# One weight load of a decode layer cut in two: seven rows for all partitions, the eighth by loads of 96, 25 and 7 partitions

## The chip, the cores and the metric

The kernel runs on one core of a Trainium2 chip. The metric is the device time of one execution in microseconds (us), taken as the median of several runs. Inputs and weights lie in HBM; everything that is computed on has to be brought into SBUF (128 partitions) by DMA first. The core has 16 DMA engines that share this work.

## The reference

One layer of a transformer decodes one new token for each of 4 sequences (hidden size D = 1024):

```
h  = x + attention(layernorm(x)) @ wo     # 32 heads of 128, 4 kv heads, the last 2048 cached positions
h2 = h + (silu(n @ w1) * (n @ w3)) @ w2   # n = layernorm(h), F = 3584
```

with q = layernorm(x) @ wq, softmax(q k^T / sqrt(128)) v per head, and everything stored in bfloat16. wq and wo are 1024 x 4096 and 4096 x 1024 (8 MB each), w1, w3 and w2 are 1024 x 3584 or 3584 x 1024 (7 MB each), the part of the k and the v cache that is read is 8 MB each. With 4 tokens per weight the work is nearly all reading: the trace counts 55.58 MB read from HBM.

## The kernel before

All big tensors pass through one SBUF tile, `ring` (128 partitions x 5 units of 16384 bfloat16), in which `at(unit, ...)` gives views: `wq_s` at unit 0, `k_s` at 3, the v blocks at 2 and 0, `wo_s` at 3, `w1_s` at 1, `w3_s` at 3, and w2 in five blocks of 13, 8, 4, 2 and 1 rows from unit 0 on. A view is overwritten by the next tensor as soon as its last reader is done, so a load may have to wait for compute.

Every load goes through `load(dst, src)` (L124), a DMA issued by SyncE (SP). SP issues them in program order: wq in two pieces, four of k, four of v, wo, w1 (L432), w3, w2 in blocks. The program order is written by hand (`tc.manual_schedule()`); each load waits for the readers of the place that it overwrites and, as eight DMA semaphores are used in turn, for an earlier load on the same semaphore.

The weights are spread so that each partition holds whole rows of a matrix:

```
w1_v = B_w1.rearrange("(p kc) f -> p kc f", kc=KC)
w1_s = at(1, KC, F)
...
load(w1_s, w1_v)
```

With KC = 8, partition p holds rows 8p to 8p+7 of w1, each 3584 values or 7168 bytes, in HBM one run of 57344 bytes. The matmuls of `up_projection` (L494) go over kc from 0 to 7, and over each half of the columns in turn; `up_projection(w1_s, ...)` makes the gate, `up_projection(w3_s, ...)` the other factor. The load of w1 stands behind `output(1)`, whose matmuls (L381) are the last readers of the v blocks that lay in w1's place.

At the end the blocks of w2 arrive one by one and are multiplied as they come: the first two into `early_ps` (L538), the last three, of which the one-row block is loaded in two halves, into `y2_ps` (L554, called y_ps in the profile). Then `res` is made (L577, L578, L582) and stored by four small DMAs (L587), two from SP and two from ScalarE.

Of the kernel before, what the change touches and what calls it, by code (L numbers as in the profile page):

```python
# [10 lines left out]
P = 128  # L11
# [10 lines left out]
def kernel(  # L22
# [29 lines left out]
    KC = D // P  # L52
# [27 lines left out]
    w1_v = B_w1.rearrange("(p kc) f -> p kc f", kc=KC)  # L80
# [17 lines left out]
    def at(unit, *shape):  # L98
        o = unit * UNIT
        view = ring[:, o : o + int(np.prod(shape))]  # L100
        if len(shape) == 1:
            return view
        names = "abc"[: len(shape)]
        return view.rearrange(
            f"p ({' '.join(names)}) -> p {' '.join(names)}", **dict(zip(names, shape))
        )
# [5 lines left out]
    w1_s = at(1, KC, F)  # L112
# [10 lines left out]
    def load(dst, src):  # L123
        nc.sync.dma_start(out=dst, in_=src)  # L124
# [216 lines left out]
    def spread(b):  # L341

        P4 = ktpool.tile([P, JR * L5, Hkv], BF16, tag="P4")
        nc.vector.tensor_tensor(  # L344
            out=P4[:],
            in0=stage.pop(("p1", b))[:].rearrange("p (x o) -> p x o", o=1).to_broadcast([P, JR * L5, Hkv]),
            in1=gmask[:].to_broadcast([P, JR * L5, Hkv]),
            op=ALU.mult,
        )
        stage[("P4", b)] = P4  # L350
# [22 lines left out]
    def output(b):  # L373
        PT = stage.pop(("PT", b))
        o_ps = (
            small[:, 0].rearrange("p (j d) -> p j d", j=JM)
            if b % 2
            else ps.tile([P, JM, Dh], FP32, tag="ktA", name="o_ps")[:]
        )
        for i in range(JR // JM):  # L380
            nc.tensor.matmul(  # L381
                o_ps,
                lhsT=PT[:, i * JM : (i + 1) * JM, :].rearrange("p j h -> p (j h)"),
                rhs=v_s[b][:, i * JM : (i + 1) * JM, :],
                start=(i == 0),
                stop=(i == JR // JM - 1),
            )
        od = act.tile([P, JM, Dh], FP32, tag="od", bufs=1)
        nc.vector.scalar_tensor_tensor(  # L389
            out=od[:],  # L390
            in0=o_ps,
            scalar=rinv[:, b : b + 1],
            in1=jmask[:].to_broadcast([P, JM, Dh]),
            op0=ALU.mult,
            op1=ALU.mult,
        )
        o2 = act.tile([P, 2, Dh], FP32, tag="o2", bufs=1)
        nc.gpsimd.tensor_tensor(out=o2[:], in0=od[:, :2], in1=od[:, 2:], op=ALU.add)  # L398
        nc.gpsimd.tensor_tensor(out=om[:, b], in0=o2[:, 0], in1=o2[:, 1], op=ALU.add)
# [29 lines left out]
    spread(2)  # L429
    transpose_p(2)  # L430
    output(1)
    load(w1_s, w1_v)  # L432
    spread(3)
    transpose_p(3)
    total(1)
# [111 lines left out]
    for k in range(2):  # L547
        part = h1[2 * R * k : 2 * R * k + 2 * R, :]
# [25 lines left out]
    for k in range(2):  # L574
        part = slice(2 * R * k, 2 * R * k + 2 * R)
# [44 lines left out]
```

## Time and profile before

| | |
|---|---|
| median of 3 runs | 138.7 us (138.65 to 138.75) |
| the profiled execution's own time | 138.7 us |
| its span, first to last instruction | 136.7 us |
| mean granted TensorE clock | 0.912 |
| read from HBM, rate over the span | 55.58 MB, 407 GB/s |
| DMA share of the chain that ended last | 59% |
| PE busy, DVE busy, ACT busy | 74.8, 49.9, 28.8 us |

The 2.0 us between the span and the time lie before the first and after the last profiled instruction. A time in the text such as 133.61 is counted from the start of the span. The profile says of each DMA how many packets it took, and each packet's start, length and size; it does not say which of the 16 engines carried a packet. A load raises its semaphore once for each engine that worked on it, when that engine's share has landed; these times are in the trace as well.

### The profile page before, as it was taken

The numbers are of one execution on the slowest core, as the hardware profiler recorded it, in microseconds if no ns is written. First come the engines' busy times: TensorE is split into PE (matmuls) and PEld (weight loads), VectorE is DVE, ScalarE is ACT, GpSimd is POOL, SyncE is SP. The second block draws the span as 40 slices with busy tenths as digits, with TensorE's granted clock in tenths as the row PEclk, the third lists the DMA queues.
The fourth block names the chain that finished last, engine by engine and source line by source line (L and its number), as shares of the span: only waits on it lengthen the run. The fifth ranks groups of instructions, "written<-read, shape, count | busy, mean of one in ns | idle before, by whom it ended". The sixth has DMA issues, their size and how long they took to land.

```text
span 136.7 us, 1762 instructions
## 1 busy us (share of the span) xinstructions
PE 74.8 (55%) x762; PEld 40.6 (30%) x762; DVE 49.9 (37%) x50; ACT 28.8 (21%) x32; POOL 15.3 (11%) x41
## 2 busy tenths in 40 slices
PE   0000044959999986029966875994184000946471
PEld 0000011439957852014423323341042000413240
DVE  0000110006526363989799920004100594090022
ACT  3000130025968495104000000000405400000000
POOL 7300060000000000000176333000200000000000
PEclk9999999999999999955999999599959955599999
DMA  4999697999999999998978979969799798999960
GB/s 163 497 454 538 269 537 307 432 417 451 408 432 436 412 436 408 436 585 360 556 326 364 556 326 475 520 285 537 336 470 508 302 520 372 384 423 432 384 245 2
DMA packets 2795, 55.70 MB, mean 408 GB/s; under 512 B 324, under 2 KB 612, under 8 KB 740
## 3 DMA queue, kind: packets, MB, share of 16 engines
q1 hardware_dynamic: 2752, 55.58, 95.3%
q8 instruction: 6, 0.10, 0.3%
q10 hardware_dynamic: 36, 0.01, 0.0%
q14 instruction: 1, 0.01, 0.0%
HBM read 55.58 MB, written 0.01 MB: 407 GB/s over the span
## 4 chain that ended last, share of the span: by engine, by line
DMA 59%; PE 28%; DVE 6%; ACT 3%; SPq 1%; issue 1%; DVEq 0%
DMA ring<-in_B_w_dram 43%; DMA ring<-in_A_wq_dram 15%; PE kt_ps L267 9%; PE sc_ps L290 5%; PE q_ps L233 4%; PE o_ps L381 4%; PE gate L494 3%; DVE P L344 2%; DVE PT L366 2%; ACT ring L271 1%; PE small L381 1%; DVE ring L269 1%; SPq L124 1%; DVE rmax L302 1%; ACT q_sb L243 1%
## 5 line engine op out<-in xcount | busy, mean ns | idle before, releaser
L271 ACT COPY ring<-kt_ps 128x2048 bf16<-128x2048 bf16 x8 | 14.6, 1866 | 7.1 <-PE kt_ps L267 7.1
L267 PE MATMUL kt_ps<-ident,ring 128*128 128x128 bf16 x256 | 15.0, 219 | 0.6 <-DVE Qm L253 0.5
L267 PEld LDWEIGHTS <-ring 128*128 128x128 bf16 x256 | 14.4, 98 | 2.6 <-issue 2.6
L269 DVE COPY ring<-kt_ps 128x2048 bf16<-128x2048 bf16 x8 | 9.8, 1225 | 9.3 <-PE kt_ps L267 9.3
L398 POOL TENSOR_TENSOR o<-od 128x256 f32<-128x256 f32 x4 | 6.8, 1695 | 54.2 <-DVE od L389 54.2
L193 PE MATMUL sums_ps<-both,mean_f 128*128 128x64 f32 x4 | 1.1, 366 | 18.9 <-ACT both L191 18.9
L494 PE MATMUL up<-ring,n_T 128*32 128x448 bf16 x64 | 4.7, 467 | 12.2 <-DMA ring<-in_B_w_dram 12.2
L494 PEld LDWEIGHTS <-n_T 128*32 128x32 bf16 x128 | 4.2, 121 | 20.2 <-DMA ring<-in_B_w_dram 12.7
L344 DVE TENSOR_TENSOR P<-p,gmask 128x2048 bf16<-128x2048 bf16 x4 | 9.1, 2278 | 0.8 <-ACT p L331 0.8
L381 PEld LDWEIGHTS <-PT 128*128 128x128 bf16 x64 | 6.7, 107 | 9.0 <-issue 1.9
L366 DVE STREAM_TRANSPOSE PT<-P 128x2048 bf16<-128x2048 bf16 x4 | 9.2, 2306 | 0.1
L515 DVE RECIPROCAL eg<-eg 128x896 f32<-128x896 f32 x1 | 5.8, 5753 | 9.5 <-ACT eg L514 9.5
L468 PE MATMUL y_ps<-ring,oP 128*32 128x512 bf16 x64 | 8.8, 442 | 0.1
L233 PE MATMUL q_ps<-ring,n_T 128*32 128x512 bf16 x64 | 6.6, 587 | 3.8 <-DMA ring<-in_A_wq_dram 2.0
L381 PE MATMUL o_ps<-ring,PT 128*128 128x512 bf16 x32 | 8.6, 430 | 0.0
L290 PE MATMUL sc_ps<-ring,Qm 128*32 128x512 bf16 x64 | 7.6, 604 | 0.4 <-DVE ring L269 0.4
L538 PE MATMUL early_ps<-ring,hg_T 128*32 128x512 bf16 x42 | 4.9, 379 | 5.1 <-DMA ring<-in_B_w_dram 5.1
L381 PE MATMUL small<-ring,PT 128*128 128x512 bf16 x32 | 7.2, 379 | 0.7 <-DVE rinv L362 0.7
L193 PEld LDWEIGHTS sums_ps<-both,mean_f 128*128 128x128 f32 x4 | 0.8, 248 | 19.4 <-issue 16.9
L494 PE MATMUL gate<-ring,n_T 128*32 128x448 bf16 x64 | 4.6, 458 | 3.2 <-DMA ring<-in_B_w_dram 3.2
L577 ACT CAST res<-y_ps 64x128 bf16<-64x128 f32 x1 | 0.3, 259 | 26.3 <-PE y_ps L554 26.3
L218 DVE STREAM_TRANSPOSE x_T<-x_nat 128x256 bf16<-128x256 bf16 x1 | 0.6, 626 | 13.0 <-DMA x_nat<-in_A_x_dram 13.0
(81 smaller groups left out, 62.5 us busy)
## 6 DMA issues: line engine op xcount, KB each, us to landing
ring<-in_B_w_dram SPq DMA_DIRECT2D x2, 7168.0 KB
ring<-in_A_k_cache_dram SPq DMA_DIRECT2D x4, 2048.0 KB, 25.6
ring<-in_A_v_cache_dram SPq DMA_DIRECT2D x4, 2048.0 KB, 42.9
ring<-in_A_wq_dram SPq DMA_DIRECT2D x1, 7168.0 KB, 21.2
ring<-in_B_w_dram SPq DMA_DIRECT2D x1, 3328.0 KB
ring<-in_B_w_dram SPq DMA_DIRECT2D x1, 2048.0 KB
ring<-in_A_wq_dram SPq DMA_DIRECT2D x1, 1024.0 KB, 4.6
ring<-in_B_w_dram SPq DMA_DIRECT2D x1, 1024.0 KB, 28.1
```

What stands on the lines that cost most here:

```text
L233: nc.tensor.matmul(q_ps[R * c : R * c + R, hf], lhsT=xn_T[:, kc, :], rhs=wq_s[:, kc, o : o + HALF * Dh], start=(kc == 0), stop=(kc == KC - 1),
L267: nc.tensor.transpose(out=kt_ps[:, jj], in_=blocks[:, jj, :], identity=ident[:])
L269: nc.vector.tensor_copy(out=blocks, in_=kt_ps[:])
L271: nc.scalar.copy(out=blocks, in_=kt_ps[:])
L290: nc.tensor.matmul(sc_ps[b // 2][R * q : R * q + R, b % 2], lhsT=Qm[:, b, g * R : (g + 1) * R], rhs=kT[:, b, g, q], start=(g == 0), stop=( ...
L344: nc.vector.tensor_tensor(out=P4[:], in0=stage.pop(("p1", b))[:].rearrange("p (x o) -> p x o", o=1).to_broadcast([P, JR * L5, Hkv]), in1=g ...
L366: nc.vector.transpose(out=PT[:].rearrange("p j h -> p (j h)"), in_=stage.pop(("P4", b))[:].rearrange("p x g -> p (x g)"),)
L381: nc.tensor.matmul(o_ps, lhsT=PT[:, i * JM : (i + 1) * JM, :].rearrange("p j h -> p (j h)"), rhs=v_s[b][:, i * JM : (i + 1) * JM, :], star ...
L398: nc.gpsimd.tensor_tensor(out=o2[:], in0=od[:, :2], in1=od[:, 2:], op=ALU.add)
L468: nc.tensor.matmul(y_ps[R * i : R * i + R], lhsT=oP[:, t, :], rhs=row[:, i], start=False, stop=(t == T - 1), tile_position=(0, R * i), ski ...
L494: nc.tensor.matmul(out_ps[hf][R * c : R * c + R, :], lhsT=hn_T[:, kc, :], rhs=cols[:, kc, c, hf], start=(kc == 0), stop=(kc == KC - 1), ti ...
L515: nc.vector.reciprocal(out=eg[:], in_=eg[:])
```

## The change

Rows 0 to 6 of every partition of w1 come by one load, row 7 by three loads, for partitions 0 to 95, 96 to 120 and 121 to 127. All four are issued by SP where the one load was. The bytes, their places and the readers are the same.

```
@@ -429,7 +429,9 @@
     spread(2)
     transpose_p(2)
     output(1)
-    load(w1_s, w1_v)
+    load(w1_s[:, : KC - 1], w1_v[:, : KC - 1])
+    for part in (slice(0, 96), slice(96, 121), slice(121, P)):
+        load(w1_s[part, KC - 1 :], w1_v[part, KC - 1 :])
     spread(3)
     transpose_p(3)
     total(1)
```

On the other engines the order of instructions stays as it was; SP has three DMA issues more, between the first piece of w1 and w3. The eight DMA semaphores are taken in turn, so the loads and stores behind w1 use a semaphore three places further on than before.

More of the change, by code (lines that the diff above doesn't have):

```diff
@@ L431 @@
     output(1)
-    load(w1_s, w1_v)
+    load(w1_s[:, : KC - 1], w1_v[:, : KC - 1])
+    for part in (slice(0, 96), slice(96, 121), slice(121, P)):
+        load(w1_s[part, KC - 1 :], w1_v[part, KC - 1 :])
     spread(3)
```

## The prediction

> **What bounds the kernel now.** I read the chain that ended last first, in order of time; its columns are start, length and what.
>
> ```profile
> 68.72 30.62 DMA ring<-in_B_w_dram
> 99.34 0.14 issue
> 99.48 4.64 PE gate L494 x55
> ...
> 104.96 28.65 DMA ring<-in_B_w_dram
> 133.61 0.04 issue
> 133.65 0.30 PE y_ps L554 x2
> 133.95 0.02 issue
> 133.97 0.43 DVE res L582
> ```
>
> The end hangs on the landing of the last half row of w2 at 133.61. The load was issued 28.65 us earlier and stood in the queue all that time: the second piece of the chain is a queue, not a transfer. So the question is when the DMA engines get through their work. The windows say how full they are (last two columns: share of 16 engines, GB/s).
>
> ```profile
> 60.00:80.00 20.00, 15.10 (x64) 6.70 (x65) 17.19 (x13) 1.56 (x4) 7.42 (x6) 0.88 1.02 440
> 80.00:97.00 17.00, 11.89 (x84) 5.27 (x82) 2.44 (x5) 1.81 (x4) 1.48 (x4) 0.90 1.01 436
> 97.00:114.00 17.00, 4.62 (x64) 2.24 (x64) 6.86 (x4) 3.53 (x5) 0.54 (x3) 0.76 1.00 432
> ```
>
> From 60 to 114 all sixteen work without a break. Narrow windows at the end show something else:
>
> ```profile
> 131.00:131.40 0.40, 0.06 (x2) 0.00 (x0) 0.30 (x1) 0.00 (x0) 0.00 (x0) 1.00 0.94 341
> 131.40:131.80 0.40, 0.13 (x8) 0.13 (x11) 0.37 (x2) 0.00 (x0) 0.00 (x0) 1.00 0.46 177
> 131.80:132.20 0.40, 0.40 (x24) 0.32 (x17) 0.16 (x1) 0.00 (x0) 0.00 (x0) 1.00 0.37 146
> 132.20:132.50 0.30, 0.30 (x8) 0.19 (x2) 0.00 (x0) 0.00 (x0) 0.00 (x0) 1.00 0.32 113
> ```
>
> A share of 0.32 is five engines of sixteen. The other eleven are through by about 131.7 and five work on until 133.1. The 16 updates of the last load's semaphore say the same: ten come at 131.75 to 132.18, one at 132.94, five at 133.47 to 133.61. Every load gives each engine the same bytes, so five engines were held up. The queues name a cause:
>
> ```profile
> q1 hardware_dynamic: 2752, 55.58, 95.3%
> q8 instruction: 6, 0.10, 0.3%
> q10 hardware_dynamic: 36, 0.01, 0.0%
> q14 instruction: 1, 0.01, 0.0%
> ```
>
> Queue 8 is instruction fetch: six packets of 16384 bytes, in the packet records at 34.1, 40.7, 50.5, 82.5, 105.6 and 132.6, each about 1.05 us long on one engine. After each of the first five, one more of the sixteen updates of every later load is late by 1.3 to 1.7 us: none in the load that lands at 32.2, one at 38.5, two at 43.4, three at 53.2, four for w1 (99.2 to 99.3, the others 97.5 to 97.9), five for w3. An engine never makes up for it, as its queue is never empty. The packet of queue 14, at 119.1, holds up a sixth engine by 1.0 us (the update at 132.94). The fetch at 132.6 falls on an engine that has finished.
>
> **The change, part by part.** *Shares.* A load is dealt out in equal shares. The counts of queue 1 fit: 19 loads of 128 rows at 8 packets and one closing packet for each of 16 engines make 2736, and the two stores from SP with 4 rows make 2 x (4 + 4) = 16, in all 2752. Queue 10 fits likewise: 36 = 2 x (4 + 4) for the stores from ScalarE and 16 + 4 for the load of x, which has 16 rows of 512 bytes in an outer dimension of 4 and closes only four times. So the engines used are as many as divide the outer dimension: by this reading 96 partitions go to 16 engines at 6 rows, 25 to 5 engines at 5 rows, 7 to 7 engines at 1 row.
> [...]
>
> If each load starts from the same engine, as I assume, the five are among the seven. Of the eighth row five engines then have 6 + 5 + 1 = 12 pieces, two have 7, nine have 6, where each had 8 pieces' worth.
>
> *Price of a piece.* In the long packets of w1, 436 GB/s over 16 is 27.25 GB/s, or 0.263 us for 7168 bytes. As a packet of its own it is nearer the 8192-byte packets of the trace, which take 0.309 to 0.314 us: 7/8 of 0.313 is 0.274. A further closing packet is 9 ns, and neighbours overlap by 4. So five engines gain 12 x 0.274 - 8 x 0.263 + 0.015 = 1.20 us of work, two lose 0.18, nine lose 8 x 0.263 - 6 x 0.274 - 0.005 = 0.46.
>
> *Issue.* SP spends 0.33 to 0.43 us on an issue; three more put its end of the w1 block from 69.1 to about 70.3. Its next instruction, w3, was issued at 93.02 (it waits for PE's y_ps), and the engines reach w1's first packets only at 80.0, behind wo. Ten microseconds hide this; uncovered it would be 1.2.
> *Semaphores.* The three extra loads move the later ones to other semaphores. The last two of w2 now also wait for pieces of w1, which land by 100 and are issued from 104.5 on; the stores at 134 wait for w3 (116.3) and older loads. Zero, with 4 us of cover at the least.
> *The gate* waits for four semaphores. PE was idle 3.20 us for w1, which lands with its slowest engine. Moved by -0.46 to +1.2, its start at 99.48 moves along; behind it DVE had eg ready at 114.36, 5.2 us before `up` let it go on, so nothing of this reaches the end.
>
> *Fixed cost of small loads.* The row: the one-row pieces of w2 (128 KB each) land 0.36 and 0.35 us apart, of which 128 KB at 436 GB/s are 0.30. So a load that stands in a full queue costs 0.05 us, three at most 0.15, and I take the closing packets alone.
> [...]
>
> *The end.* It follows the last landing one for one: 0.04 + 0.30 + 0.43 and the stores lie behind it, and PE waited for each piece of w2 (1.82 us before the second block, 0.61, 0.28), so it isn't the bound 0.5 us earlier either. All hangs on which engines get 12 pieces. If they are five of the ten that are on time, these land at 132.95 to 133.38 and the late five at 133.01 to 133.15. Nine of the ten on-time updates lie at or below 131.96, so most choices end at 133.16 and only the one at 132.18 makes it 133.38: a gain of 0.23 to 0.46. I take 0.40. The profiled execution's 138.7 is the median, so 138.3.
>
> Are they on time? The packets of x (queue 10, 6.7 to 13.2) mark four streams that a small outer dimension uses, and packets follow one another on an engine at -3 or -4 ns, so streams can be followed by joining ends to starts. The streams hit at 40.7 and 82.5 are not among the four in any joining that fits. Those of 34.1, 50.5 and 105.6 run level with others at times and stay open, the first two more likely outside than in. This makes it likelier than a blind choice that the late five are spared, not sure.
>
> **The rivals.**
> *A late engine is loaded.* One of the five is among those with 12 pieces. It ends 1.2 later: 133.61 + 1.2 = 134.8, 139.9. One is enough, whatever the rest do. For it: three of five streams can't be told apart from the four marked ones. Against: two can, and those hit seem to lie on one side. Chance 0.28.
> *The engine of the 119.1 fetch, or of the one at 132.6, is loaded,* and none of the five. The first lands at 132.94 + 1.2 = 134.14, 139.2. The second would end near 132.6, as the fetch comes, and be pushed by some 1.0 to 133.6 or a little later, with landing 134.1. Chance 0.13.
> *No effect:* the shares of 25 and 7 are dealt over all sixteen, so that each has about 8, or gains and losses meet: 138.7. Chance 0.05.
> *The small loads cost* 0.05 each on every engine, 0.15, and eat a third of the gain, or their fixed cost shows: 138.5 up. By the rows they stand in a full queue. Chance 0.03. [...]
> *One engine takes all 25:* 25 x 0.274 - 2 x 0.263 = 6.3 later, 145. Against: a load of 4 rows goes to four. Chance 0.02.
>
> **How the numbers follow.** Forecast 0.49: 138.15 to 138.5, of which a little falls within 0.2% (0.28 us, what a measurement here can tell from no change). Faster 0.46; same 0.09 (the no-effect case and the edge of the forecast); slower 0.45. Range 138.1 to 139.95: it leaves out only the last rival and the far end of the fourth. Forecast and both loaded-engine cases lie in it, 0.9 together; to shorten it would drop a case of 0.28.
>
> **What would show it.** Right: the share at the end falls from near 1 to 0 within about 0.8 us, later than 131.4 and by 133; last landing near 133.2; w1's last landing near 98.9; the 25-partition load with five updates from engines. Wrong: a tail with fewer engines (1 to 4 of 16, a share near 0.06 to 0.25) until 134.3 means that loaded engines were late ones; six updates spread as before means no effect; gaps in the DMA share around 97 mean fixed costs.

## The result and the profile after

The change made the kernel slower: 143.37 us (143.04 to 143.76, 4 runs) against 138.68, a ratio of 1.034 with a 95% interval of 1.0305 to 1.0374. The forecast was 138.3 with a range to 139.95. The profiled execution took 143.76 us, its span is 141.7. Of the runs further down, one of 161.21 us fell into a slower state of the chip and is left out.

The chain that ended last (start, length, what) has the same shape as before; what differs is when the loads land.

```profile
69.44 34.08 DMA ring<-in_B_w_dram
103.52 0.14 issue
103.66 1.94 PE gate L496 x34
...
106.48 31.94 DMA ring<-in_B_w_dram
138.42 0.04 issue
138.47 0.30 PE y_ps L556 x2
138.77 0.02 issue
138.79 0.43 DVE res L584
```

The last half row lands at 138.42 instead of 133.61, 4.81 later, which is nearly all of the 5.06 us between the two profiled executions. w1 lands complete at 103.52 instead of 99.34, so 4.2 us are lost by then.

The windows of the changed kernel around these loads (five lines, then the kernel before from 95 to 103 in one line; the last two columns are DMA share and GB/s; a packet is counted in the window in which it starts):

```profile
80.00:94.00 14.00, 11.38 (x82) 4.93 (x79) 0.94 (x2) 0.27 (x1) 1.17 (x2) 0.88 1.02 438
...
95.00:97.00 2.00, 0.44 (x2) 0.30 (x2) 0.55 (x2) 1.62 (x3) 0.38 (x3) 1.00 0.82 194
97.00:99.00 2.00, 0.00 (x0) 0.00 (x0) 0.37 (x2) 0.30 (x2) 0.46 (x3) 0.95 1.79 337
99.00:101.00 2.00, 1.87 (x24) 0.93 (x28) 0.00 (x0) 0.00 (x0) 0.00 (x0) 0.50 0.60 104
101.00:103.00 2.00, 0.94 (x12) 0.13 (x4) 0.00 (x0) 0.00 (x0) 0.00 (x0) 0.70 1.21 384
...
95.00:103.00 8.00, 3.96 (x50) 2.11 (x54) 1.00 (x4) 1.93 (x4) 0.84 (x4) 0.79 0.93 401
```

Up to 94 the seven rows come at 438 GB/s. From 95 to 103 the four windows average 255 GB/s at an average share of 1.1: all sixteen engines are busy and move little more than half of that. The kernel before moved 401 in this stretch. The packet records say the same. A packet of 7168 bytes takes 0.272 us in the first moments, then 0.55, later 0.6 to 0.84; the median is 0.558. It isn't these packets alone: the seven packets of w3 that start from 97.7 to 98.6 take 4.8 to 5.1 us instead of 2.12, and the last packets of the seven rows on the four streams that were late take 2.8 to 3.25 instead of 1.86. Nine more packets of w3, which start from 101.3 to 102.2 as the short loads run out, take 2.7 to 3.3. Packets that start after 103 have their old lengths again.

The sum per engine is 4.43 us for the pieces of the eighth row (all 128 packets over 16) where 8 x 0.263 = 2.10 was paid before, 1.80 more for w3's packets and 0.36 more for the seven rows: 4.5 us in the mean of the engines. The updates of the last load agree roughly: the mean of the sixteen moved from 132.48 to 136.75, by 4.3.

The packet count is what the shares of the prediction give:

```profile
q1 hardware_dynamic: 2908, 55.58, 95.0%
```

2908 - 2752 = 156 = (96 + 16) + (25 + 5) + (7 + 7): one packet a row, and 16, 5 and 7 closing packets.

The tail at the end is still there, with ten engines in it (share 0.59) instead of five, and a last one by itself:

```profile
136.00:136.40 0.40, 0.00 (x0) 0.00 (x0) 0.37 (x2) 0.00 (x0) 0.00 (x0) 1.00 0.59 210
136.40:136.80 0.40, 0.33 (x18) 0.33 (x21) 0.39 (x1) 0.00 (x0) 0.00 (x0) 1.00 0.58 202
136.80:137.20 0.40, 0.40 (x20) 0.29 (x9) 0.00 (x0) 0.00 (x0) 0.00 (x0) 1.00 0.08 28
137.20:137.60 0.40, 0.26 (x2) 0.11 (x2) 0.00 (x0) 0.00 (x0) 0.00 (x0) 1.00 0.25 64
137.60:138.00 0.40, 0.25 (x12) 0.25 (x12) 0.00 (x0) 0.00 (x0) 0.00 (x0) 1.00 0.05 18
```

The updates of the last load tell these apart: six come by 136.10, nine from 137.13 to 137.48, and one at 138.42. The packet records show what parted the last one from the nine: the instruction packet of queue 14 starts at 119.67, just as the last of the ten streams ends its last packet of w3, and the packet of w2 behind it takes 1.64 us instead of 0.99. So 3.9 of the 4.81 us are common to the late streams (133.61 to 137.48), and the other 0.94 is that fetch. In the kernel before it held up a stream with time to spare (132.94).

### The profile page after: what moved, and what is told of

The parts are those of the page before. It is cut to its first block, busy times and chain, and to the rows that moved or that the text cites. A ratio compares the mean times of both kernels' runs of the same rounds, so it can differ in the third digit from the quotient of the medians.

```text
span 141.7 us, 1768 instructions
## 1 busy us (share of the span) xinstructions
PE 77.4 (55%) x762; PEld 41.3 (29%) x762; DVE 50.0 (35%) x50; ACT 28.8 (20%) x32; POOL 15.3 (11%) x41
## 3 DMA queue, kind: packets, MB, share of 16 engines
q1 hardware_dynamic: 2908, 55.58, 95.0%
## 4 chain that ended last, share of the span: by engine, by line
DMA 62%; PE 25%; DVE 6%; ACT 3%; SPq 1%; issue 1%; DVEq 0%
DMA ring<-in_B_w_dram 47%; DMA ring<-in_A_wq_dram 15%; PE kt_ps L267 9%; PE sc_ps L290 5%; PE q_ps L233 4%; PE o_ps L381 3%; DVE P L344 2%; DVE PT L366 2%; PE gate L496 1%; ACT ring L271 1%; SPq L124 1%; PE small L381 1%; DVE ring L269 1%; DVE rmax L302 1%; ACT q_sb L243 1%
## 5 line engine op out<-in xcount | busy, mean ns | idle before, releaser
L496 PE MATMUL up<-ring,n_T 128*32 128x448 bf16 x64 | 5.6, 537 | 15.6 <-DMA ring<-in_B_w_dram 15.6
L540 PE MATMUL early_ps<-ring,hg_T 128*32 128x512 bf16 x42 | 6.6, 476 | 2.5 <-DMA ring<-in_B_w_dram 2.5
```

The costliest lines, as they stand in the source:

```text
L496: nc.tensor.matmul(out_ps[hf][R * c : R * c + R, :], lhsT=hn_T[:, kc, :], rhs=cols[:, kc, c, hf], start=(kc == 0), stop=(kc == KC - 1), ti ...
L540: nc.tensor.matmul(early_ps[R * i : R * i + R], lhsT=hg_T[:, fc, :], rhs=row[:, i], start=(fc == 0), stop=(fc == FE - 1), tile_position=(0 ...
```

## The experiments

In all of them only the load of w1 is changed, but for the last. Shown is what stands in place of the one load. "Part 1" is the load of seven rows for all partitions, `load(w1_s[:, : KC - 1], w1_v[:, : KC - 1])`.

The theories at first: (1) the partitions of these loads are dealt to the engines so that several write the same part of SBUF; (2) short rows at a stride are slow to read in HBM; (3) only the uneven shares cost.

**One load for the eighth row.**

```
 part 1
+load(w1_s[:, KC - 1 :], w1_v[:, KC - 1 :])
```

> Seven rows for all partitions, then the eighth by one load of 128 partitions: same bytes, even shares, no partition split. Theory 1 (the odd partition splits make several DMA engines write the same part of SBUF and slow each other): the 7168-byte packets take 0.27 us as in their first moments, time 138.7 to 139.0. Theory 2 (short rows read at a stride of 57344 bytes are slow in HBM): the 7168-byte packets take 0.5 to 0.6 us, 8 x 0.3 us more per engine, time 141 to 141.6. Theory 3 (only the uneven number of rows per engine costs): 138.7 to 139.0 as theory 1.

Measured: 139.0 us, ratio 1.0018 (1.0007 to 1.003). The 7168-byte packets take 0.275 us, none over 0.287. So neither the short row, nor its stride of 57344 bytes, nor a second load costs anything to speak of: theory 2 falls. The full rate holds through the place where the change loses it:

```profile
97.00:99.00 2.00, 0.99 (x22) 0.55 (x26) 0.37 (x2) 0.40 (x2) 0.55 (x3) 0.99 1.37 584
99.00:101.00 2.00, 2.00 (x28) 0.96 (x24) 0.00 (x0) 0.00 (x0) 0.00 (x0) 0.50 0.99 430
```

**96 and 32 partitions, even shares.**

```
 part 1
+for part in (slice(0, 96), slice(96, P)):
+    load(w1_s[part, KC - 1 :], w1_v[part, KC - 1 :])
```

> As the change, but the last row by loads of 96 and 32 partitions, so that all 16 engines get 6 + 2 rows. Theory 1: packets of the 96-partition load slow as in the changed kernel (0.4 to 0.6 us), 140.5 to 141.5. Theory 2: the same, 141 to 141.6. Theory 3 (uneven shares): 138.7 to 139.0.

Measured: 142.6 us, ratio 1.0265 (1.0234 to 1.0296); median packet 0.532 us. Every engine has its 8 pieces, and most of the loss is there. Theory 3 falls; the loss was larger than theory 1 had said, as w3's first packets slow down too (3.3 to 3.7 us).

```profile
95.00:97.00 2.00, 0.43 (x2) 0.30 (x2) 0.41 (x2) 1.72 (x4) 0.53 (x3) 1.00 0.92 229
97.00:99.00 2.00, 0.00 (x0) 0.00 (x0) 0.37 (x2) 0.21 (x1) 0.32 (x2) 0.63 0.93 165
```

**All of w1 by 96 and 32 partitions,** in packets of 57344 bytes.

```
+for part in (slice(0, 96), slice(96, P)):
+    load(w1_s[part], w1_v[part])
```

> Whole w1 (all eight rows, packets of 57344 bytes) by loads of 96 and 32 partitions: no short rows, no stride, but the odd partition split for all of w1. Theory 1: its packets take about 4 us instead of 2.1, w1 takes up to 17 us more, time 150 or more. Theories 2 and 3: 138.7 to 139.0.

Measured: 157.93 us. Long packets suffer as short ones do: those that start from 82 to 106 take 4.3 us in the median and up to 4.9 instead of 2.12, with all engines busy at half rate for 24 us (the kernel before moved 448 GB/s in this stretch):

```profile
82.00:106.00 24.00, 9.01 (x78) 4.50 (x78) 2.40 (x7) 2.19 (x5) 2.02 (x6) 0.79 1.07 228
```

**The change, reading neighbouring rows of HBM.**

```
 part 1
+for part in (slice(0, 96), slice(96, 121), slice(121, P)):
+    load(w1_s[part, KC - 1 :], B_w1[part].rearrange("p (o f) -> p o f", o=1))
```

> As the change (96, 25 and 7 partitions), but the last row of each partition is read from the first 128 rows of w1, which lie next to each other in HBM, so it holds other weights than the reference has there. Theory 1: slow as the change, 143 to 143.7. Theory 2: packets near 0.27 us and the balance of the prediction can show, 138.2 to 139.9. Theory 3: 143 to 143.7.

Measured: 143.24 us, ratio 1.0311 (1.0281 to 1.0341); median packet 0.538. The place in HBM makes no difference here (143.24 us against 143.37 for the change), so the cause is looked for on the side of SBUF. Theory 1 stands, but not yet what makes a set of partitions slow.

**Two halves; a middle half; four sixteenths and a half; even and odd partitions.** Part 1, and then

```
last64_64:  (slice(0, 64), slice(64, P))
mid64:      (slice(32, 96), slice(0, 32), slice(96, P))
by16:       (slice(64, 80), slice(80, 96), slice(96, 112), slice(112, P), slice(0, 64))
stride2:    (slice(0, P, 2), slice(1, P, 2))
```

> Last row by loads of partitions 0 to 63 and 64 to 127; every engine gets 4 + 4 rows. [...] Theory 1c (counts that are no power of two, as 96, 25 and 7, are the trouble): 0.275 us, 138.8 to 139.1.

> Last row by loads of partitions 32 to 95, then 0 to 31, then 96 to 127. [...] Theory 1c: all near 0.275, 138.8 to 139.2.

> Last row by four loads of 16 neighbouring partitions (64 to 127), then one of partitions 0 to 63. [...] Theory 1c: 0.275 everywhere, 138.9 to 139.3.

> [...] Theory 1c: 138.8 to 139.1.

Measured: `last64_64` 143.54 us (ratio 1.0333), median packet 0.56; `mid64` 141.55 (1.0189), taken in sixteens by their start the packets have medians of 0.276, 0.276, 0.276, 0.281 and then 0.55, 0.53, 0.54, 0.46; `by16` 142.99 (1.0293), the first sixteen at 0.28, the others at 0.49 to 0.63; `stride2` 139.08, ratio 1.0009 (0.9997 to 1.0022), all at 0.27 to 0.29. From 95 to 103 `last64_64` and then `stride2`, same counts and same bytes:

```profile
95.00:103.00 8.00, 3.24 (x30) 1.36 (x30) 1.21 (x4) 1.93 (x4) 0.84 (x4) 0.69 0.99 229
...
95.00:103.00 8.00, 3.12 (x34) 1.69 (x38) 1.65 (x5) 1.93 (x4) 0.85 (x4) 0.71 1.07 455
```

The first sixteen packets of 7168 bytes have a median of 0.276 us in every run that has such packets, whichever partitions they write; only the later ones tell. Why is not known. Count and split are cleared: 64 partitions at a step of two (0.27 to 0.29 us), or 32 to 95 (0.276 to 0.281), run at full rate where 0 to 63 run at half (0.56). It is the place, and theory 1c falls with `last64_64`. `last64_64` lost 4.6 us and `mid64` 2.6, more than their slow packets add by an estimate from these medians: 8 x (0.56 - 0.275) = 2.3 and 4 x (0.52 - 0.275) = 1.0 for each engine. The rest is put down to the loads beside them, as w3's first packets took 3.3 to 3.7 us in `last96_32`. What sets the slow partitions apart these runs don't show.

**48 to 79 first; 16 to 111 first; the change's shares at a step.** As all slow loads lie in one half of the partitions or mostly so, a theory 2a came up: half the rate for each half.

```
mid32:   (slice(48, 80), slice(0, 48), slice(80, P))
mid96:   (slice(16, 112), slice(0, 16), slice(112, P))
spread:  (slice(0, P, 2), slice(1, P, 4), slice(3, 103, 4), slice(103, P, 4))
```

> Last row by loads of partitions 48 to 79, then 0 to 47, then 80 to 127. Theory 2a (each half of the partitions, 0 to 63 and 64 to 127, takes about half of the full rate; a load that lies unevenly over the halves slows all engines): the first load has 16 partitions in either half, its 32 packets stay near 0.275 us, the other 96 near 0.55, time 142 to 143. [...]

> Last row by loads of partitions 16 to 111, then 0 to 15, then 112 to 127: the change's first short load with the same 96 rows over 16 engines, but 48 in either half. Theory 2a: its 96 packets near 0.275 us, only the 32 of the two others slow, time 139.8 to 141. [...] A theory that the count of 96 itself is slow: 0.55, 142 to 143.

> The change's shares (12, 7 and 6 pieces an engine) with partitions taken at a step, so that the halves get about equal parts: the even partitions (64), every fourth from 1 (32), 25 at a step of four from 3, the last 7 at that step. Theory 2a: 64 and 32 at full speed; while five engines do the 25 and the others go on with w3, the halves are a little uneven (10 writers to 6), packets 0.3 to 0.4 us; the forecast's balance shows and loses part of its 0.4 us again: 138.2 to 139.2, the ends of the streams closer together than before. A theory that loads on fewer than 16 engines are slow as such: 140 to 141.5.

Measured: `mid32` 143.75 us (ratio 1.0365), the first 16 packets at a median of 0.28, the next 16 at 0.52 to 0.88; `mid96` 143.08 (1.0316), slow from its second row on (0.4 to 0.56), though 48 of its rows lie in either half. Theory 2a falls with `mid96`.

`spread` has the 12, 7 and 6 pieces of the change without its neighbouring partitions: 140.57, ratio 1.0134 (1.0117 to 1.0151). Its packets run at 0.275 us until five and seven engines do the last 32 rows; from then on they take 0.41 to 0.47, and the seven packets of w3 that run beside them 3.04 to 3.08; the sum above comes to 1.1 us an engine, of which `one128` has 0.2. The time lies in the range of the theory that loads on fewer than 16 engines are slow as such (140 to 141.5), which this run doesn't refute.

**Each load by itself.** Ahead of the unchanged kernel, run once, 25 loads one after the other, told apart by their packet size:

```
+for i, (lo, hi, step) in enumerate(probes):
+    width = UNIT - 128 * i
+    load(at(2, UNIT)[lo:hi:step, :width], rows[lo:hi:step, :width])
+    load(at(2, UNIT)[:, :512], rows[:, :512])
```

> Ahead of the kernel, 25 loads of w1 into a place that is overwritten later, each after the one before has landed (a 128-partition load of 1024 bytes a row stands between), with 26 to 32 KB a row, so that packets tell their load by their size. Alone and undisturbed a packet moves about 27 bytes a ns. Partitions in question: 0-127; 0-63; 32-95; 64-127; 48-79; 16-111; 0-95; even ones; every second of 16-111; every fourth; every eighth; every fourth of 32-95; every fourth of 0-63; 0-15; 56-71; 0-7; 64-71; every fourth of 0-31; every fourth of 64-95; 0-24; 96-120; 121-127; 8-119; 0-31; 0-127. [...] Theory 2a (half the rate for each half of the partitions): full for 0-127, 32-95, 48-79, 16-111, 8-119, 56-71, every set at a step over all 128 and every load on 5, 7 or 8 engines; half for 0-63, 64-127, 0-31, 0-15, every fourth of 0-63. Theory 3 (engines 0 to 7 have their path to partitions 0 to 63, the others to 64 to 127; what crosses is slow): as 2a, but 64-71, every fourth of 64-95, 96-120 and 121-127 slow as well.

The bytes of each load over the time from its first packet's start to its last one's end:

```
partitions                     rows   engines  GB/s
0-127 (first, last)            128    16       392, 378
32-95                          64     16       344
even ones                      64     16       350
every fourth                   32     16       294
every fourth of 32-95          16     16       225
0-63; 64-127                   64     16       194; 194
48-79; 0-31                    32     16       181; 178
every eighth                   16     16       172
every fourth of 0-63           16     16       183
0-15; 56-71                    16     16       113; 113
0-7; 64-71                     8      8        69; 63
121-127                        7      7        66
every fourth of 0-31; of 64-95 8      8        119; 122
0-95; 16-111; every second     96,48  16       205; 210; 219
8-119                          112    16       246
0-24; 96-120                   25     5        115; 112
```

The short loads hold some start-up in these rates. Neither engines nor rows alone set the rate: loads on 16 engines moved 113 to 392 GB/s, 64 rows 194 or 344 to 350, 32 rows 178 to 294. Neighbouring partitions are slow in most cases (63 and 69 for 8, 113 for 16, 178 and 181 for 32, 194 for 0 to 63 and for 64 to 127), but 32 to 95 (344) goes nearly like 0 to 127, where 48 to 79 (181) goes like 0 to 31 (178). A step doesn't help as such: every eighth partition moved 172. What sets a slow set apart from a fast one no run shows beyond these sets. Loads of 25 rows are at full speed when nothing else runs (27 bytes a ns on each of five engines), so a load on five engines isn't slow as such. Theories 2a and 3 had 48 to 79 at the full rate; it moved 181 GB/s, which is against both. The windows of this run, over 0 to 63, 32 to 95, 64 to 127, 16 to 111 and the even partitions, again count by starts:

```profile
18.00:26.00 8.00, 0.00 (x0) 0.00 (x0) 0.00 (x0) 0.00 (x0) 0.00 (x0) 1.00 0.96 195
32.50:36.50 4.00, 0.00 (x0) 0.00 (x0) 0.00 (x0) 0.00 (x0) 0.00 (x0) 1.00 0.90 387
42.00:50.00 8.00, 0.00 (x0) 0.00 (x0) 0.00 (x0) 0.00 (x0) 0.00 (x0) 1.00 0.94 192
...
70.00:76.00 6.00, 0.00 (x0) 0.00 (x0) 0.00 (x0) 0.00 (x0) 0.00 (x0) 1.00 1.08 236
103.00:106.00 3.00, 0.00 (x0) 0.00 (x0) 0.00 (x0) 0.00 (x0) 0.00 (x0) 1.00 1.03 444
```

The share is near 1 in all five rows while the rate differs by more than a factor of two: the engines count as busy while they are held up. That it is the writing that holds them up is the author's inference from `contig` (143.24 us with neighbouring rows of HBM); this view doesn't show it.

## Why the prediction was wrong

*Failed: the price of a piece.* The prediction took 0.274 us for a row of 7168 bytes from the 8192-byte packets of the trace, all of which belong to loads of 128 partitions. Size was the only thing it carried over. The pieces of the change took 0.55 in the mean (4.43 x 16 / 128). What it left out is which partitions a load writes: by itself the load of 0 to 95 moved 205 GB/s and that of 121 to 127 moved 66, while that of 96 to 120 was at full speed (112 GB/s on five engines) and slow only beside the others: in the change no packet of 7168 bytes that starts after 98.5 takes under 0.48 us, and the five updates of this load come at 101.72 to 102.98. That engines which write certain partitions at once hold each other up is the author's reading; no view shows it. And the term had no share for others: w3 and part 1, which the prediction left alone, paid 2.2 of the 4.5 us.

*Failed as well: that no loaded engine meets the fetch of queue 14.* The forecast of 138.3 needs this, and the rival of the engine of the 119.1 fetch (139.2, part of a chance of 0.13) says otherwise. In the three runs with these shares (the change, `contig` and `spread`) ten streams are late at the end and the last stands 0.94, 1.06 and 0.83 us behind the next. In the kernel before and in the runs with even shares the stream that queue 14 holds up is one that was on time, and the last two updates are at most 0.21 apart. If the packet goes to the same engine each time, which the trace doesn't name, that engine is one of the loaded five. Then 138.3 would have been missed at the predicted price as well.

*Failed with it: the list of rivals.* It looked for a cost in the number of loads and in the shares. `one128` and `stride2` show that one or two added loads in a full queue cost 0.1 to 0.2 us in all. The far end of the fourth rival, which the range left out, needs a larger fixed cost of a small load; no run shows one. No rival asked what a load's partitions do to the rate. "A late engine is loaded" had the sign; it was not what happened.

*Right: what bounds the kernel.* The end still follows the last landing (138.42, with 0.30 and 0.43 us of work behind it), and each engine's queue decides it.

*Right: the shares.* 16, 5 and 7 closings, and the load of 25 has five updates, that of 7 has seven. That both start from the same engine, on which the 12 pieces rest, was the author's assumption: the runs show these counts, and no view names the engines.

*Right: none of the late five is loaded.* The updates of the four late streams for the 96 partitions come at 102.36 to 103.15; five more rows at 0.6 would end after 105. All five updates of the 25-row load come at 101.72 to 102.98, so none of these four carries it. The fifth, held up at 107.4, can only be counted. At the end six updates come at 135.54 to 136.10 and ten at 137.12 to 138.42: as many as neither loaded nor late, and as loaded and late together. The loaded five did come up to the late ones. The late ones did not gain; everything moved back.

*Argued, not shown: that moving rows cannot help here.* Say that how fast a row is written goes with its partition and not with its engine: then a row moved to another engine meets the same neighbours as before, and the late engine loses by company what it is relieved of. This is the author's conjecture. `spread` fits: same shares, 1.1 us lost per engine. But the loads of 8 neighbours moved 63 and 69 GB/s, more than two engines' 27 each, so one engine alone does not take up what 8 neighbouring partitions can. Whether moved rows could use the moment in which an engine is held by an instruction fetch was not tried. No run beat the kernel before; the best, `one128` and `stride2`, equal it within 0.2%.

*Right, and harmless:* issue, semaphores, gate. w3 was issued at 92.94 where 93.02 was read before, so the three issues stayed hidden. The later gate (103.66) put the next issues of w2 at 104.63 to 106.48 without emptying the queue.

## What to carry to other kernels

A price per packet holds only for the partitions it was measured on (here 0.276 us for 32 to 95, 0.56 for 0 to 63 and 64 to 127): before a load is split by partitions, measure the piece by itself and beside the loads it will run with. Splits along the free dimension (`one128`, ratio 1.0018) and into even and odd partitions (`stride2`, 1.0009) cost next to nothing here; steps of four with uneven shares (`spread`) cost 1.3%. A load of partitions 0 to 63 ran at 194 GB/s alone, half the 392 of 0 to 127, one of 32 to 95 at 344. Here the sign of it was a DMA share near 1 with a rate of some 200 GB/s in place of 430.

## What the runs showed of the hardware

Each of the first five fetches of instructions leaves one of the 16 engines 1.3 to 1.7 us behind, and it doesn't recover while the queue is full; in the kernel before, five fetches leave five streams late at the end. Where a further fetch falls decides what it costs: the one of queue 14 cost nothing on a stream with time to spare, and 0.94 us on a loaded one.

The short loads of the change slowed what ran beside them: the seven packets of w3 that began from 97.7 to 98.6, in their middle, took 4.8 to 5.1 us instead of 2.12. Whether this meets every engine or some alone can't be told, as the trace does not name the engines.

How much a set of partitions can take is measured only for the sets of the last experiment. Why 0 to 95 and 16 to 111 move 205 and 210 GB/s, little more than the 194 of 0 to 63, where 0 to 127 moves 378 to 392, stays open, and with it the size of the change's loss.

How rows are dealt to engines is open as well, beyond the counts of updates (16, 5 and 7): no view names the engine of a packet.
